# V's scale on GpSimd, and ten score products in one TensorE group

## The chip, the cores and the metric

The program runs on one core of one Trainium2 chip, as a single launch. The metric is the device time of one execution in microseconds, as a median of several runs. The profile is of one further execution. Engines are named as the profile names them: PE (TensorE matmul), PEld (its weight loads), DVE (VectorE), ACT (ScalarE), POOL (GpSimd), SP (SyncE, which issues the DMAs).

## The reference

There are two stages, for 8 batches of 576 positions. The first is causal attention in a window of 128 with 8 heads of 64 and a bias that falls with distance; the second is a gated MLP in which positions are mixed by a matrix.

```
scores = q @ k.T / 8 + slope[h] * -(i - j), kept where 0 <= i - j < 128
attn   = softmax(scores);  x = attn @ v, heads side by side     # 576 x 512 per batch
h      = relu(x @ w_in);   u, v = halves of h                   # 512 each
v_n    = (v - mean(v)) / sqrt(var(v) + 1e-6)
v_s    = w_spatial @ v_n + b_spatial
out    = (u * v_s) @ w_out
```

## The kernel before

**Tiling.** Heads are worked on in pairs (head 2p in partitions 0 to 63, head 2p+1 in 64 to 127), so a batch has four pairs. The 576 positions make five tiles of queries: four of 128 and one of 64. Tile t needs only the keys of tiles t-1 and t, so its scores are 128 wide (tile 0), 256 (tiles 1 to 3) or 192 (tile 4). Batch 1, and the first pair of batch 2, go through another path (`raw_tile`, lines 416 to 487), which the change leaves alone. The other 27 pairs go through `attention(b, p)`, line 500.

**One pair in `attention`.** The scores are fp32 products of 64 rows (L520, one per tile and head), put into PSUM banks tagged "s", of which there are four; two tiles of one head share a bank. `PIECES` cuts them into two groups on PE: tiles 0 to 3 of both heads, and later tile 4, which again takes two "s" banks. DVE adds the bias table and takes the row minimum (L531), ACT takes the exponential and its sum (L537), DVE makes the reciprocals (L545, L549), ACT and DVE split the scaled probabilities into two fp16 halves (L557, L562), and SP issues a DMA transpose of them (L568).

**V's scale.** V is split into two fp16 halves after scaling by a power of two. ACT takes the row sums of |V| (L579, "the abs" below, which writes into the buffer `vl` and into `am`). PE transposes these 128 sums into one row of a PSUM bank tagged "x" (L583), DVE takes the largest and clamps it (L587, L588), PE spreads it to all partitions by two products with a row of constants (L593), DVE makes powers of two of it (L599, L600), and then V is scaled and split (L604 or L607, and L611).

**P times V.** 84 small fp16 products per pair (L624; the trace merges them to 42 rows), in two banks tagged "x", of which there are two in all. ACT and DVE take the result out as two halves of `xt` (L633, L637).

**The MLP of a batch** (`gated`). All its products go through two PSUM banks tagged "m". First five units of v (L689 for a tile of 128, L711 for the tile of 64): relu on ACT (L271) into `vt`, of which there are two buffers, then the statistics on DVE (L650, L654, L655), the power -1/2 on POOL (L659, "the power" below), the scaling on DVE (L663) and the split (L267, L700). Then eight units each of u (L741, 12 products), of the mixing (L762, 14 products; L770 and L776 gate its result) and of the output (L788, 12 products; L267 copies its result out).

**What sets the order.** Nothing is decided at run time. A planner (`Plan`, lines 46 to 135) takes each piece of work with a weight in ns, a due time and its reads and writes, replays them on a clock of its own and writes each engine's queue in that order. Each engine then works its own queue strictly in that order, with semaphores between engines. So work of the attention of one batch stands among the MLP units of the batch before, and a buffer of a tag is handed on in the order in which the pieces were added to the plan.

Of the kernel before, what the change touches and what calls it, by code (L numbers as in the profile page):

```python
# [138 lines left out]
def attn_gmlp_kernel(ctx, tc, qk, v, w_in, w_spT, b_sp, w_out, outT):  # L139
# [48 lines left out]
    def pe(*cols):  # L188
        return sum(11 + n / 2.4 for n in cols)
# [4 lines left out]

    nhalf = fixed([P, 1], F32, "nhalf")
    ident = fixed([P, P], F32, "ident")
    ones = fixed([1, 2 * P], BF16, "ones")
# [26 lines left out]
    def constants():  # L224
        def f():
            nc.gpsimd.iota(relf(), [[-1, 2 * P]], base=P, channel_multiplier=1, allow_small_or_imprecise_dtypes=True)
        plan.add("POOL", 400, 0, f, (), [(relf, 0)])

        def f():
            nc.vector.memset(maskt(), 0.0)  # L230
        plan.add("DVE", dve(256), 0, f, (), [(maskt, 0)])

        def f():
            nc.gpsimd.affine_select(maskt(), maskt(), [[-1, 2 * P]], ALU.is_ge, MASKED, base=P, channel_multiplier=1)
            nc.gpsimd.affine_select(maskt(), maskt(), [[1, 2 * P]], ALU.is_ge, MASKED, base=-1, channel_multiplier=-1)
        plan.add("POOL", 800, 1, f, [(maskt, 0)], [(maskt, 0)])

        def f():
            nc.vector.memset(ident(), 1.0)
            nc.vector.memset(ones()[:, :P], 2.0 ** -12)  # L240
            nc.vector.memset(ones()[:, P:], 2.0 ** -13 / PSC)
            nc.vector.memset(nhalf(), -0.5)
            nc.vector.memset(rstat(), 1.0)
        plan.add("DVE", dve(400), 500, f, (), [(ident, 0), (ones, 0), (nhalf, 0)] + [(rstat, k) for k in range(8)])
# [255 lines left out]
    def attention(b, p):  # L500

        due = FIRST + b * PERIOD - LEAD - (NP - 1 - p) * PERIOD // 4
        st = stat[p % 2]
# [3 lines left out]
        if (b, p) in RAW:  # L507
            xt = plan.buf(work, "xt", 6, [P, 2 * S + R], F32R)
            for t in range(NQ):
                raw_tile(b, p, t, raw, vr, xt, t % 4, due - 6000 + t * 1500)  # L510
            return xt
        for g, banks in enumerate(PIECES):
            sc = [[plan.buf(ps, "s", 4, [P, 2, 2 * P], F32) for _ in range(2)] for _ in banks]
            span = [(k, i, t, min(P, S - t * P), max(0, (t - 1) * P), min(S, (t + 1) * P)) for k, ts_ in enumerate(banks) for i, t in enumerate(ts_)]

            def f(sc=sc, span=span):
                for k, i, t, m, k0, k1 in span:
                    for j in range(2):
                        rows = slice(j * D, (j + 1) * D)
                        nc.tensor.matmul(sc[k][j]()[:m, i, :k1 - k0], raw()[rows, 0, t * P:t * P + m], raw()[rows, 1, k0:k1],  # L520
                                         start=True, stop=True)
            plan.add("PE", SWITCH + pe(*[4 * (x[5] - x[4]) for x in span]), due - 5000 + g * 3000, f, RAWS,
                     [(sc[k][j], i) for k, i, *_ in span for j in range(2)])
            for k, i, t, m, k0, k1 in span:
                for j in range(2):
                    h, n, c0 = 2 * p + j, k1 - k0, P if t == 0 else 0
                    pt = lambda j=j, m=m, t=t, n=n: prob[j]()[:m, OFF[t]:OFF[t] + n]
                    d = due - 4500 + t * 700 + j * 200

                    def f(sc=sc[k][j], pt=pt, i=i, j=j, h=h, t=t, m=m, n=n, c0=c0):  # L530
                        nc.vector.tensor_tensor_reduce(pt(), sc()[:m, i, :n], tabs[h]()[:m, c0:c0 + n], -0.125, 3e38,  # L531
                                                       ALU.add, ALU.min, st()[:m, NM, j, t:t + 1])
                    cols = parts(prob[j], OFF[t], OFF[t] + n)
                    plan.add("DVE", dve(n), d, f, [(sc[k][j], i), (tabs[h], 0)], cols + [(st, (NM, j, t))])

                    def f(pt=pt, j=j, t=t, m=m):
                        nc.scalar.activation(pt(), pt(), AF.Exp, bias=st()[:m, NM, j, t:t + 1], scale=-1.0,  # L537
                                             accum_out=st()[:m, SM, j, t:t + 1])
                    plan.add("ACT", act(n, 2), d, f, cols + [(st, (NM, j, t))], cols + [(st, (SM, j, t))])
        pts = []  # L540
        for j in range(2):
            d = due + j * 1500
# [25 lines left out]
                nc.sync.dma_start_transpose(out=pts[j](), in_=pq[j]().rearrange("p a b -> p (a b)"))  # L568
            plan.add("SP", 3400, d + 1500, f, parts(pq[j], 0, 2 * NB * P), [(pts[j], 0)])


        vh, vl = (plan.buf(work, tag, 2, [P, NQ, P], F16) for tag in ("vh", "vl"))
        am = plan.buf(work, "am", 2, [P, 8], F32)
        one = plan.buf(work, "one", 2, [1, 2], BF16)
        mp = plan.buf(ps, "x", 2, [P, 512], F32)
        d = due - 3000

        def f():
# [1 line left out]
        plan.add("ACT", act(NQ * P, 1), d, f, VRS, [(vl, 0), (am, 0)])  # L580

        def f():
            nc.tensor.transpose(mp()[0:1, 0:P], am()[:, 0:1], ident())  # L583
        plan.add("PE", SWITCH // 2, d + 1, f, [(am, 0), (ident, 0)], [(mp, 0)])

        def f():
            nc.vector.tensor_reduce(one()[:, 0:1], mp()[0:1, 0:P], AX.X, ALU.max)  # L587
            nc.vector.tensor_scalar(one()[:, 0:1], one()[:, 0:1], 2.0 ** -98, 2.0 ** 126, ALU.max, ALU.min)  # L588
        plan.add("DVE", 400, d + 2, f, [(mp, 0)], [(one, 0)])

        def f():
            for k in range(2):
                nc.tensor.matmul(mp()[:, P + k:P + k + 1], ones()[:, k * P:(k + 1) * P], one()[:, 0:1], start=True, stop=True,  # L593
                                 skip_group_check=True)
# [230 lines left out]
    def first(t):  # L825
        for p in range(NP) if t < NQ else ():
            raw_tile(0, p, t, *loads[p], x0[p], p, 2000 + t * 6500 + p * 1500)
        if 0 <= t - 2 < NC_:
            c = t - 2
            win_weights(0, c, UDUE[c], w_u[c])  # L830

    gated(0, x0, first)
    for b in range(1, B):
        xt = []
        for p in range(NP):
            if b == 1 and (b, p) not in RAW and (b, p - 1) in RAW:
                clear()
            xt.append(attention(b, p))
        gated(b, xt)
    plan.emit()  # L840


# [30 lines left out]
```

## Time and profile before

| | |
|---|---|
| median of 3 runs | 648.48 us (648.08 to 651.25) |
| the profiled execution | 648.05 us; its span from first to last instruction 646.3 us |
| granted PE clock, mean | 0.992 of full speed |
| PE busy | 619.0 us, 96% of the span |
| DVE, ACT, POOL busy | 524.2 (81%), 430.9 (67%), 29.6 us (5%) |
| one batch, from the third on | 72.97 us, alike to 0.02 us from batch to batch |

A busy time is the union of an engine's instructions, so it tells how long an engine had something to do and not how well it did it. In the timeline a row gives start, length, engine, line, operation, output and inputs, size and count; rows that follow each other on the same line are merged. Because the rows of PE overlap, what a group costs is read from its start to the start of the next group.

### The profile page before, as it was taken

How to read it: one execution, taken by the hardware profiler on the slowest of the kernel's cores; microseconds unless marked ns; L12 is line 12 of the kernel's file. 1: busy time of each engine (PE TensorE's matmuls, PEld its weight loads, DVE VectorE, ACT ScalarE, POOL GpSimd, SP SyncE). 2: the span in 40 equal slices, each digit the busy share in tenths (PEclk: the TensorE clock that was granted, in tenths of full speed). 3: DMA queues.
4: the chain of work that ended last, by engine and by line, in shares of the span. 5: the costliest groups of instructions: out<-in, count | busy, mean ns of one | idle time of the engine just before them, and what ended most of it. 6: DMA issues, size and time to landing. Idle time of an engine off the chain costs nothing.

```text
span 646.3 us, 14141 instructions
## 1 busy us (share of the span) xinstructions
PE 619.0 (96%) x5037; PEld 529.8 (82%) x5037; DVE 524.2 (81%) x1897; ACT 430.9 (67%) x1322; POOL 29.6 (5%) x53
## 2 busy tenths in 40 slices
PE   4879999999999999999999999999999999999997
PEld 2445688778899879988898979988898978988997
DVE  6999898999887979887887979887887979873632
ACT  4698675989585848686686848676686857662211
POOL 1000010000200010000100010000100010000100
PEclk9998799999999999999999999999999999999999
DMA  7903013799156863778165753858166751733001
GB/s 264 329 20 130 19 62 119 169 209 202 55 132 133 190 107 93 155 155 184 40 143 127 191 112 89 154 152 188 32 154 125 193 113 10 132 79 76 2 20 55
DMA packets 149291, 79.34 MB, mean 123 GB/s; under 512 B 128610, under 2 KB 139874, under 8 KB 149220
## 3 DMA queue, kind: packets, MB, share of 16 engines
q1 hardware_dynamic: 149220, 78.44, 51.8%
q8 instruction: 39, 0.64, 0.4%
q14 instruction: 32, 0.26, 0.1%
HBM read 37.13 MB, written 9.44 MB: 72 GB/s over the span
## 4 chain that ended last, share of the span: by engine, by line
PE 79%; DVE 17%; issue 1%; DMA 1%; ACT 1%; SPq 1%; ACTq 0%; DVEq 0%
PE m L762 16%; PE m L741 16%; PE m L788 14%; PE m L689 13%; PE s L520 8%; PE x L624 6%; DVE pq L562 4%; PE m L711 2%; DVE prob L436 2%; DVE prob L531 2%; DVE gs L298 1%; DMA pt<-in_qk_dram 1%; DVE prob L450 1%; DVE u L770 1%; DVE o L267 1%
## 5 line engine op out<-in xcount | busy, mean ns | idle before, releaser
L537 ACT ACTIVATE prob<-prob,stat 128x128 f32<-128x128 f32 (+1 forms) x270 | 125.4, 466 | 13.6 <-DVE stat L531 12.4
L762 PE MATMUL m<-wsp,vn 128*128 128x288 f32 x768 | 124.3, 299 | 0.7 <-DVE u L770 0.7
L788 PE MATMUL m<-gs,wout 128*128 128x288 f32 x768 | 113.5, 301 | 0.3 <-DVE gs L776 0.2
L762 PEld LDWEIGHTS m<-wsp,vn 128*128 128x128 f32 x768 | 107.5, 188 | 6.7 <-issue 1.9
L557 ACT ACTIVATE pq<-prob,stat 128x128 f16<-128x128 f32 x270 | 103.1, 464 | 12.7 <-ACT prob L537 10.2
L741 PE MATMUL m<-xt,win 128*128 128x288 f32 x768 | 111.6, 298 | 0.0
L788 PEld LDWEIGHTS m<-gs,wout 128*128 128x128 f32 x768 | 103.3, 188 | 7.2 <-issue 1.7
L562 DVE SCALAR_TENSOR_TENSOR pq<-prob,stat,pq 128x128 f16<-128x128 f32 x270 | 104.0, 437 | 4.3 <-ACT pq L557 3.7
L741 PEld LDWEIGHTS m<-xt,win 128*128 128x128 f32 x768 | 103.9, 188 | 4.1 <-issue 2.3
L689 PE MATMUL m<-win,xt 128*128 128x512 f32 x384 | 93.5, 396 | 1.7 <-DVE o L267 1.7
L531 DVE CUSTOM_DVE_ANT_0 prob<-s,tab 128x128 f32<-128x128 f32 (+1 forms) x270 | 89.2, 376 | 2.6 <-PE s L520 2.1
L689 PEld LDWEIGHTS m<-win,xt 128*128 128x128 f32 x384 | 71.5, 189 | 18.2 <-DVE o L267 2.8
L520 PE MATMUL s<-qkraw 64*128 64x256 f32 (+2 forms) x540 | 66.5, 360 | 1.5 <-DVE stat L531 1.3
L770 DVE TENSOR_TENSOR u<-m,u 128x288 f32<-128x288 f32 x64 | 28.9, 451 | 34.2 <-PE m L762 34.2
L520 PEld LDWEIGHTS s<-qkraw 64*128 64x128 f32 (+1 forms) x540 | 42.0, 175 | 16.2 <-issue 9.0
L659 POOL TENSOR_TENSOR st<-st,nhalf 128x1 f32<-128x1 f32 (+1 forms) x40 | 25.6, 640 | 560.4 <-DVE st L655 548.0
L537 ACT ACTIVATION_READ_ACCUMULATOR prob<-prob,stat 128x1 f32 x270 | 50.6, 187 | 0.0
L267 ACT COPY o<-m 128x288 f32<-128x288 f32 x37 | 14.6, 395 | 46.2 <-PE m L788 45.9
L624 PE MATMUL x<-pt,vh 128*64 128x256 f16 (+6 forms) x756 | 41.7, 229 | 0.0
L271 ACT ACTIVATE vt<-m 128x512 f32<-128x512 f32 x31 | 18.5, 598 | 33.0 <-DVE st L654 16.1
L637 DVE SCALAR_TENSOR_TENSOR xt<-x,am,xt 128x288 fp32r<-128x288 f32 x54 | 26.2, 507 | 17.1 <-ACT xt L633 17.0
L624 PEld LDWEIGHTS <-vh 128*64 128x64 f16 x756 | 31.7, 110 | 5.8 <-issue 3.5
(132 smaller groups left out, 820.7 us busy)
## 6 DMA issues: line engine op xcount, KB each, us to landing
qkraw<-in_qk_dram SPq DMA_DIRECT2D x28, 576.0 KB, 3.9
out_dram<-o SPq DMA_DIRECT2D x64, 144.0 KB, 2.0
vraw<-in_v_dram SPq DMA_DIRECT2D x28, 320.0 KB, 2.9
vn<-in_w_in_dram SPq DMA_DIRECT2D x6, 512.0 KB, 7.1
pt<-in_w_out_dram SPq DMA_DIRECT2D x4, 512.0 KB, 4.5
gs<-in_w_spT_dram SPq DMA_DIRECT2D x4, 288.0 KB, 5.0
xt<-in_w_in_dram SPq DMA_DIRECT2D x2, 512.0 KB, 6.8
qkraw<-in_qk_dram SPq DMA_DIRECT2D x3, 320.0 KB, 8.3
```

What stands on the lines that cost most here:

```text
L520: nc.tensor.matmul(sc[k][j]()[:m, i, :k1 - k0], raw()[rows, 0, t * P:t * P + m], raw()[rows, 1, k0:k1], start=True, stop=True)
L531: nc.vector.tensor_tensor_reduce(pt(), sc()[:m, i, :n], tabs[h]()[:m, c0:c0 + n], -0.125, 3e38, ALU.add, ALU.min, st()[:m, NM, j, t:t + 1])
L537: nc.scalar.activation(pt(), pt(), AF.Exp, bias=st()[:m, NM, j, t:t + 1], scale=-1.0, accum_out=st()[:m, SM, j, t:t + 1])
L557: nc.scalar.activation(pq[j]()[:m, 0, cs], prob[j]()[:m, cs], AF.Copy, scale=st()[:m, RC, j, t:t + 1])
L562: nc.vector.scalar_tensor_tensor(pq[j]()[:m, 1, cs], prob[j]()[:m, cs], st()[:m, RC, j, t:t + 1], pq[j]()[:m, 0, cs], ALU.mult, ALU.subtract)
L624: nc.tensor.matmul(xp()[j * D:(j + 1) * D, x0:x0 + n], l()[:, kt, j * D:(j + 1) * D], rhs[:, o:o + n], start=j not in seen, stop=False, sk ...
L637: nc.vector.scalar_tensor_tensor(xt()[:, S + R + hf * HS:S + R + (hf + 1) * HS], xp()[:, :HS], am()[:, 6:7], xt()[:, qs].bitcast(F32), ALU ...
L689: nc.tensor.matmul(pt(), xt[c]()[:, X0[a] + t * P:X0[a] + (t + 1) * P], win()[:, c, w, DH:DF], start=(n == 0), stop=(n == 3 * NC_ - 1))
L741: nc.tensor.matmul(pt()[:, :HS], win()[:, c, w, d * P:(d + 1) * P], xt[c]()[:, X0[a] + hf * HS:X0[a] + (hf + 1) * HS], start=(n == 0), sto ...
L762: nc.tensor.matmul(pt()[:, :HS], l, r, start=(n == 0), stop=(n == len(ops) - 1))
L770: nc.vector.tensor_tensor(u(), pt()[:, :HS], u(), ALU.mult)
L788: nc.tensor.matmul(pt()[:, :HS], wout()[:, d, w, e * P:(e + 1) * P], gs[d]()[:, a, :], start=(n == 0), stop=(n == 3 * ND - 1))
```

## The change

Three things are changed, and the planner's order follows from them.

1. V's scale no longer goes through PE and PSUM. POOL takes the largest of the 128 sums and spreads it, in one instruction (`partition_all_reduce`, weight 4000 in the plan), and DVE does the clamping and the powers of two in four small instructions.
2. From batch 3 on (24 pairs) the ten scores of a pair are one group on PE. Tile 4's two scores go to the two "x" banks, which P times V also uses. The three pairs of batch 2 keep two groups, in "s" banks.
3. The plan adds the scores of pair p+1 ahead of V's scale and P times V of pair p (`AHEAD`), which sets the order in which the "x" banks are handed on.

```diff
-    PIECES = (((0, 1), (2, 3)), ((4,),))
+    BANKS = (((0, 1), ("s", 4)), ((2, 3), ("s", 4)), ((4,), ("x", 2)))
...
-                    d = due - 4500 + t * 700 + j * 200
+                d = due - 4500 + (t if len(banks) < 3 or t < NQ - 1 else -1) * 700 + j * 200
...
+        for g, banks in enumerate((BANKS,) if b >= WHOLE else (BANKS[:2], ((BANKS[2][0], ("s", 4)),))):
+            products(p, due, st, raw, RAWS, g, banks)
...
-            nc.tensor.transpose(mp()[0:1, 0:P], am()[:, 0:1], ident())
-        plan.add("PE", SWITCH // 2, d + 1, f, [(am, 0), (ident, 0)], [(mp, 0)])
-
-        def f():
-            nc.vector.tensor_reduce(one()[:, 0:1], mp()[0:1, 0:P], AX.X, ALU.max)
-            nc.vector.tensor_scalar(one()[:, 0:1], one()[:, 0:1], 2.0 ** -98, 2.0 ** 126, ALU.max, ALU.min)
-        plan.add("DVE", 400, d + 2, f, [(mp, 0)], [(one, 0)])
-
-        def f():
-            for k in range(2):
-                nc.tensor.matmul(mp()[:, P + k:P + k + 1], ones()[:, k * P:(k + 1) * P], one()[:, 0:1], start=True, stop=True,
-                                 skip_group_check=True)
-        plan.add("PE", SWITCH, d + 3, f, [(one, 0), (ones, 0)], [(mp, 1)])
+            nc.gpsimd.partition_all_reduce(am()[:, 1:2], am()[:, 0:1], P, bass.bass_isa.ReduceOp.max)
+        plan.add("POOL", 4000, d + 1, f, [(am, 0)], [(am, 2)])
 
         def f():
             bits = 0x7F800000
-            nc.vector.tensor_scalar(am()[:, 5:7].bitcast(I32), mp()[:, P:P + 2].bitcast(I32), bits, None, ALU.bitwise_and)
+            nc.vector.tensor_scalar(am()[:, 2:3], am()[:, 1:2], 2.0 ** -98, 2.0 ** 126, ALU.max, ALU.min)
+            nc.vector.tensor_scalar(am()[:, 2:3].bitcast(I32), am()[:, 2:3].bitcast(I32), bits, None, ALU.bitwise_and)
+            nc.vector.tensor_scalar(am()[:, 5:7], powers(), am()[:, 2:3], None, ALU.mult)
             nc.vector.tensor_scalar(am()[:, 5:6].bitcast(I32), am()[:, 5:6].bitcast(I32), bits, None, ALU.bitwise_xor)
-        plan.add("DVE", 150, d + 4, f, [(mp, 1)], [(am, 1)])
+        plan.add("DVE", 400, d + 4, f, [(am, 2), (powers, 0)], [(am, 1)])
...
+            todo.append((b, p, scores(b, p)))
+            if len(todo) > AHEAD:
+                rest(*todo.pop(0))
```

The line numbers of the changed kernel are a little higher: L660 there is L659 before, L690 is L689, L712 is L711, L625 is L624, L589 is the abs (L579), L275 is the relu (L271), L271 is the copy (L267), L608 is L607, and L634 and L566 are L633 and L557. The all-reduce is L593 there, and the score products are L514.

How the order moves is seen at three places. The first is POOL's queue over one batch in the middle of the program, before:

```order
L659 TENSOR_TENSOR st<-st,nhalf 128x1
L659 TENSOR_TENSOR st<-st,nhalf 64x1
L659 TENSOR_TENSOR st<-st,nhalf 128x1 x4
L659 TENSOR_TENSOR st<-st,nhalf 64x1
L659 TENSOR_TENSOR st<-st,nhalf 128x1 x4
```

and in the changed kernel:

```order
L660 ISA
L660 TENSOR_TENSOR st<-st,nhalf 128x1
L660 TENSOR_TENSOR st<-st,nhalf 64x1
L660 TENSOR_TENSOR st<-st,nhalf 128x1 x3
L593 ISA
L593 ISA am<-am 128x1 x4
L660 ISA
```

The rows `ISA` without operands are put in by the build: each swaps the library of routines that POOL's cores have loaded, because the power and the all-reduce are in different ones. There is one such row in the program before, ahead of its first iota (L226); the changed program has fourteen more, two for each of seven batches, one behind a batch's fifth power and one ahead of the next batch's first. They wait for no semaphore.

The second place is PE's queue where one batch's outputs end and the next batch's v units begin, before (the first row is the last product of P times V):

```order
L624 MATMUL x<-pt,vl 64x64
L788 MATMUL m<-gs,wout 128x288 x24
L583 MATMUL x<-ident,am 1x128
L689 MATMUL m<-win,xt 128x512 x12
L593 LDWEIGHTS ones
L593 MATMUL x<-one,ones 128x1
L593 LDWEIGHTS ones
L593 MATMUL x<-one,ones 128x1
L711 MATMUL m<-win,xt 128x512 x8
L689 MATMUL m<-win,xt 128x512 x12
```

and in the changed kernel:

```order
L625 MATMUL x<-pt,vl 64x64
L690 MATMUL m<-win,xt 128x512 x12
L712 MATMUL m<-win,xt 128x512 x8
L690 MATMUL m<-win,xt 128x512 x24
L514 MATMUL s<-qkraw 128x128 x2
L514 MATMUL s<-qkraw 128x256 x6
L514 MATMUL x<-qkraw 64x192 x2
L690 MATMUL m<-win,xt 128x512 x12
L625 LDWEIGHTS vh
```

The tiny products are gone, two output units have moved ahead of P times V, and the scores with tile 4 in the "x" banks stand one v unit ahead of the next P times V.

The third place is ACT's queue at the same spot, before:

```order
L633 ACTIVATE xt<-x,am 128x288 x2
L557 ACTIVATE pq_86<-prob_84,stat_87 128x256
L557 ACTIVATE pq_86<-prob_84,stat_87 64x192
L267 COPY xt<-xt 128x64
L579 ACTIVATE vl,am<-vraw 128x640
L267 COPY o<-m 128x288
L271 ACTIVATE vt<-m 128x512
```

and in the changed kernel:

```order
L634 ACTIVATE xt<-x,am 128x288 x2
L566 ACTIVATE pq_86<-prob_84,stat_87 128x256 x2
L271 COPY xt<-xt 128x64
L566 ACTIVATE pq_86<-prob_84,stat_87 64x192
L589 ACTIVATE vl,am<-vraw 128x640
L275 ACTIVATE vt<-m 128x512
L271 COPY vt<-m 64x512
L275 ACTIVATE vt<-vt 64x512
L608 ACTIVATE vh<-vraw,am 128x640
```

The abs still stands right ahead of the first v unit's relu, but a scaling of V (L608) that DVE did there before (L604) now stands on ACT behind that unit.

More of the change, by code (lines that the diff above doesn't have):

```diff
@@ L165, in attn_gmlp_kernel @@
     PERIOD, FIRST, LEAD = 66000, 36000, 18000
+    AHEAD = 1
+    WHOLE = 2
     RAW = {(0, p) for p in range(4)} | {(1, p) for p in range(1)}
@@ L196, in attn_gmlp_kernel @@
     ident = fixed([P, P], F32, "ident")
-    ones = fixed([1, 2 * P], BF16, "ones")
+    powers = fixed([P, 2], F32, "powers")
     tabs = [fixed([P, 2 * P], BF16, f"tab{h}") for h in range(H)]
@@ L239, in f @@
             nc.vector.memset(ident(), 1.0)
-            nc.vector.memset(ones()[:, :P], 2.0 ** -12)
-            nc.vector.memset(ones()[:, P:], 2.0 ** -13 / PSC)
+            nc.vector.memset(powers()[:, 0:1], 2.0 ** -12)
+            nc.vector.memset(powers()[:, 1:2], 2.0 ** -13 / PSC)
             nc.vector.memset(nhalf(), -0.5)
             nc.vector.memset(rstat(), 1.0)
-        plan.add("DVE", dve(400), 500, f, (), [(ident, 0), (ones, 0), (nhalf, 0)] + [(rstat, k) for k in range(8)])
+        plan.add("DVE", dve(400), 500, f, (), [(ident, 0), (powers, 0), (nhalf, 0)] + [(rstat, k) for k in range(8)])
         def f():
@@ L492, in clear, with products, f @@
                      [k for a in range(2) for k in parts(pq[j], a * NB * P + OFF[NQ - 1], (a + 1) * NB * P)])
-    PIECES = (((0, 1), (2, 3)), ((4,),))
+    BANKS = (((0, 1), ("s", 4)), ((2, 3), ("s", 4)), ((4,), ("x", 2)))
     WINDOWS = (((0, 0, 256, 0), (1, 256, 160, 128), (2, 512, 32, 256)),
                ((1, 416, 96, 0), (2, 544, 224, 0), (3, 768, 192, 96), (4, 1024, 64, 224)))
-    def attention(b, p):
+    def products(p, due, st, raw, RAWS, g, banks):
+        SM, NM, RC, TM = range(4)
+        sc = [[plan.buf(ps, *tag, [P, 2, 2 * P], F32) for _ in range(2)] for _, tag in banks]
+        span = [(k, i, t, min(P, S - t * P), max(0, (t - 1) * P), min(S, (t + 1) * P)) for k, (ts_, _) in enumerate(banks) for i, t in enumerate(ts_)]
+        def f():
+            for k, i, t, m, k0, k1 in span:
+                for j in range(2):
+                    rows = slice(j * D, (j + 1) * D)
+                    nc.tensor.matmul(sc[k][j]()[:m, i, :k1 - k0], raw()[rows, 0, t * P:t * P + m], raw()[rows, 1, k0:k1],
+                                     start=True, stop=True)
+        plan.add("PE", SWITCH + pe(*[4 * (x[5] - x[4]) for x in span]), due - 5000 + g * 3000, f, RAWS,
+                 [(sc[k][j], i) for k, i, *_ in span for j in range(2)])
+        for k, i, t, m, k0, k1 in span:
+            for j in range(2):
+                h, n, c0 = 2 * p + j, k1 - k0, P if t == 0 else 0
+                pt = lambda j=j, m=m, t=t, n=n: prob[j]()[:m, OFF[t]:OFF[t] + n]
+                d = due - 4500 + (t if len(banks) < 3 or t < NQ - 1 else -1) * 700 + j * 200
+                def f(sc=sc[k][j], pt=pt, i=i, j=j, h=h, t=t, m=m, n=n, c0=c0):
+                    nc.vector.tensor_tensor_reduce(pt(), sc()[:m, i, :n], tabs[h]()[:m, c0:c0 + n], -0.125, 3e38,
+                                                   ALU.add, ALU.min, st()[:m, NM, j, t:t + 1])
+                cols = parts(prob[j], OFF[t], OFF[t] + n)
+                plan.add("DVE", dve(n), d, f, [(sc[k][j], i), (tabs[h], 0)], cols + [(st, (NM, j, t))])
+                def f(pt=pt, j=j, t=t, m=m):
+                    nc.scalar.activation(pt(), pt(), AF.Exp, bias=st()[:m, NM, j, t:t + 1], scale=-1.0,
+                                         accum_out=st()[:m, SM, j, t:t + 1])
+                plan.add("ACT", act(n, 2), d, f, cols + [(st, (NM, j, t))], cols + [(st, (SM, j, t))])
@@ L502, in attention, with scores @@
+    def scores(b, p):
         due = FIRST + b * PERIOD - LEAD - (NP - 1 - p) * PERIOD // 4
@@ L510, in attention @@
                 raw_tile(b, p, t, raw, vr, xt, t % 4, due - 6000 + t * 1500)
[L511 to L527, printed above, removed]
-                    d = due - 4500 + t * 700 + j * 200
[L530 to L539, printed above, removed]
+            return lambda: xt
+        for g, banks in enumerate((BANKS,) if b >= WHOLE else (BANKS[:2], ((BANKS[2][0], ("s", 4)),))):
+            products(p, due, st, raw, RAWS, g, banks)
         pts = []
@@ L569, in attention @@
             plan.add("SP", 3400, d + 1500, f, parts(pq[j], 0, 2 * NB * P), [(pts[j], 0)])
+        return lambda: attention(p, due, vr, VRS, pts)
+    def attention(p, due, vr, VRS, pts):
         vh, vl = (plan.buf(work, tag, 2, [P, NQ, P], F16) for tag in ("vh", "vl"))
         am = plan.buf(work, "am", 2, [P, 8], F32)
-        one = plan.buf(work, "one", 2, [1, 2], BF16)
-        mp = plan.buf(ps, "x", 2, [P, 512], F32)
         d = due - 3000
@@ L830, in first, with rest @@
             win_weights(0, c, UDUE[c], w_u[c])
+    xts = []
+    def rest(b, p, f):
+        xts.append(f())
+        if p == NP - 1:
+            gated(b, [xts.pop(0) for _ in range(NP)])
     gated(0, x0, first)
+    todo = []
     for b in range(1, B):
-        xt = []
         for p in range(NP):
@@ L837, in attn_gmlp_kernel @@
                 clear()
-            xt.append(attention(b, p))
-        gated(b, xt)
+            todo.append((b, p, scores(b, p)))
+            if len(todo) > AHEAD:
+                rest(*todo.pop(0))
+    while todo:
+        rest(*todo.pop(0))
     plan.emit()
```

## Prediction

> **What bounds the kernel now.** I read the page's busy times first (they stand in the table above), then a table of stretches (one batch, from its first power to the next batch's), then PE's timeline inside that batch, then the waits.
>
> ```profile
> 378.56:451.53 72.97, 72.54 (x621) 63.57 (x620) 61.04 (x224) 52.13 (x163) 3.17 (x6) 1.00 0.58 133
> ```
>
> The columns are the stretch and its length, then busy time of PE, PEld, DVE, ACT and POOL, PE's clock and the DMA share. PE is busy for 72.54 of 72.97 us at full clock: a batch lasts as long as PE's queue does, so a us taken from that queue is a us gained as long as nobody comes late. DVE follows with 61.04 us, and POOL has 3.17. The waits of PE on DVE for a bank are short today (engine, line, releaser, total us, times, longest):
>
> ```profile
> PE m L689 <- DVE o L267: 1.7, 4, 0.4
> PE s L520 <- DVE stat L531: 1.3, 2, 0.8
> ```
>
> **Part 1: what leaves PE.** A group's cost is read from its start to the next start.
>
> ```profile
> 325.44 0.56 PE L762 MATMUL m<-wsp,vn 128*128 128x288 f32 x3
> ...
> 327.28 1.75 PE L741 MATMUL m<-xt,win 128*128 128x288 f32 x12
> ...
> 342.00 0.27 PE L583 MATMUL x<-ident,am 128*1 128x128 f32 x1
> 342.03 0.65 PE L762 MATMUL m<-wsp,vn 128*128 128x288 f32 x3
> ...
> 344.06 0.20 PE L593 MATMUL x<-one,ones 1*128 1x1 bf16 x2
> 344.19 1.86 PE L788 MATMUL m<-gs,wout 128*128 128x288 f32 x12
> 345.98 1.79 PE L520 MATMUL s<-qkraw 64*128 64x128 f32 x16
> 347.70 1.85 PE L788 MATMUL m<-gs,wout 128*128 128x288 f32 x12
> ...
> 352.88 0.54 PE L520 MATMUL s<-qkraw 64*64 64x192 f32 x4
> 353.36 1.86 PE L788 MATMUL m<-gs,wout 128*128 128x288 f32 x12
> ```
>
> ```profile
> 309.04 5.78 PE L689 MATMUL m<-win,xt 128*128 128x512 f32 x24
> 314.74 1.79 PE L520 MATMUL s<-qkraw 64*128 64x128 f32 x16
> ...
> 368.63 3.44 PE L788 MATMUL m<-gs,wout 128*128 128x288 f32 x24
> 371.91 0.27 PE L583 MATMUL x<-ident,am 128*1 128x128 f32 x1
> 372.61 3.03 PE L689 MATMUL m<-win,xt 128*128 128x512 f32 x12 [0.43 <-DVE o L267]
> 375.58 0.20 PE L593 MATMUL x<-one,ones 1*128 1x1 bf16 x2
> 375.71 2.11 PE L711 MATMUL m<-win,xt 128*128 128x512 f32 x8
> 377.65 1.54 PE L689 MATMUL m<-win,xt 128*128 128x512 f32 x6
> ```
>
> First, what a change of shape costs at its ends. An output unit between two other shapes takes 345.98 - 344.19 = 1.79 us (a unit and two ends). Two units behind P times V and ahead of L583 take 371.91 - 368.63 = 3.28 us (two units and one end, since L583 turns out to cost the unit ahead of it nothing). So a unit is 1.59 us and an end 0.10 us. A mixing unit among its like takes 327.28 - 325.44 = 1.84 us, but 344.06 - 342.03 = 2.03 us between L583 and L593: 0.10 is L593's end, 0.09 belongs to L583.
>
> - L583: 342.03 - 342.00 = 0.03, and 0.09 in the unit behind, 0.12 us.
> - L593: 344.19 - 344.06 = 0.13, and two ends, 0.33 us; where it touches a score group (one pair in four in this batch) only 0.13. Mean 0.28 us.
> - Both for 27 pairs: 27 x 0.40 = 10.8 us.
> - Tile 4 as a group of its own: 353.36 - 352.88 = 0.48 and two ends, 0.68 us. In the large group it costs its columns: the 16 rows of tiles 0 to 3 take 347.70 - 345.98 = 1.72 us for 896 columns per head, so 192 columns take 0.37 us. Saved 0.31 us, less where a tiny product shares the end: 0.28 us x 24 pairs = 6.7 us.
>
> Together 17.5 us, all of it on the path. The DVE instructions of V's scale stay four small ones, so I count nothing there; they are covered by DVE's 11.9 idle us per batch, and if that cover were gone they would cost what they cost before. DMAs: none is added, and the order of SP's queue moves outputs and loads of q, k and v past each other by a place or two; I count nothing, since the DMA engines are busy for 0.58 of the batch.
>
> **Part 2: tile 4 in the "x" banks.** P times V of one pair now waits until DVE has read tile 4's scores of the next pair, and those scores wait until P times V of the pair before has been taken out. In the v stage the order leaves one v unit between the scores and P times V. Nothing like it is in the trace. Below: nothing, since two output units moved ahead of P times V loosen another wait. Above: the longest wait of PE on DVE, 0.8 us, for each of 24 pairs, 19 us. I take one mean wait per batch (1.7 + 1.3 over 6 waits, 0.5 us) for six batches: 3 us, because DVE has a sixth of its time free and tile 4 is put first in its queue.
>
> **Part 3: POOL's two swaps of library.** This decides the sign. Each batch's queue is now: five powers, swap, four all-reduces, swap. The second swap starts when the last all-reduce ends and stands ahead of the next batch's first power. Behind that power waits DVE's scaling L663, and behind L663 all of DVE's queue. The rows at that place, from ACT, DVE and POOL:
>
> ```profile
> 372.38 0.73 ACT L579 ACTIVATE vl<-vraw 128x640 f16<-128x640 f32 x1
> 373.02 0.19 ACT L579 ACTIVATION_READ_ACCUMULATOR vl<-vraw 128x1 f32 x1
> ...
> 375.68 0.60 ACT L271 ACTIVATE vt<-m 128x512 f32<-128x512 f32 x1 [2.19 <-PE m L689]
> ```
>
> ```profile
> 379.15 0.55 DVE L663 TENSOR_SCALAR vt<-vt,st 128x512 f32<-128x512 f32 x1
> ...
> 380.68 0.67 DVE L700 TENSOR_TENSOR vn<-vt,vn 128x512 fp32r<-128x512 f32 x1
> ```
>
> ```profile
> 378.56 0.55 POOL L659 TENSOR_TENSOR st<-st,nhalf 128x1 f32<-128x1 f32 x1 [60.95 <-DVE st L655]
> ```
>
> The abs ends at 373.21, 4.6 us behind the end of P times V (368.63), and ACT's order there has not changed. In the changed order the first v unit starts right at the end of P times V; call that 0. The power starts no earlier than 4.6 + R + S, with R the all-reduce and S the swap. Unit 1's `vt` is free at L700's end, 381.35 - 378.56 = 2.8 us behind the power's start, and then unit 3's relu takes 0.6. PE needs that relu's bank for unit 5, which it reaches after 2.97 (372.61 to 375.58), 1.94 (L711), 5.70 (309.04 to 314.74) and the joined scores (1.72 + 0.37): 12.7 us. So PE loses 4.6 + R + S + 3.4 - 12.7 = S + R - 4.7 us per batch, and nothing below that. The last batch has no scores in that place: 2.1 us more.
>
> R: nearest is the power on the same 128x1 operand, 0.55 us; I take 0.6, with 0.3 and 1.0 as ends, other POOL rows. S is in no row as a number of its own. What there is:
>
> ```profile
> 0.90 0.34 POOL L226 IOTA u<- 128x256 f32 x1 [0.39 <-POOLq L861]
> ```
>
> ```profile
> vn<-in_w_in_dram SPq DMA_DIRECT2D x6, 512.0 KB, 7.1
> pt<-in_w_out_dram SPq DMA_DIRECT2D x4, 512.0 KB, 4.5
> gs<-in_w_spT_dram SPq DMA_DIRECT2D x4, 288.0 KB, 5.0
> xt<-in_w_in_dram SPq DMA_DIRECT2D x2, 512.0 KB, 6.8
> qkraw<-in_qk_dram SPq DMA_DIRECT2D x3, 320.0 KB, 8.3
> ```
>
> The only swap of before sits ahead of the iota, which idled 0.39 us: the lower end. But the program before needs one library only, so that swap may have found it loaded by the execution before. [...] I take the mean of the three that landed among other traffic, (7.1 + 6.8 + 8.3) / 3 = 7.4 us, because these swaps come in the middle of transfers too. Then PE loses 7.4 + 0.6 - 4.7 = 3.3 us in six batches and 5.4 in the last, 25 us. DVE comes out of the stall with its queue late, and PE's next waits (P times V behind the scores) come on top: 0.5 us, the mean wait above, in seven batches, 3.5 us.
>
> The first swap, behind the fifth power, delays the next all-reduce; its DVE instructions stand far behind in DVE's queue, behind the next scores, so I count nothing. If that cover is thin, it costs up to S once more.
>
> [...]
>
> **Sum.** Against the profiled execution (648.05 us: span 646.3 and 1.75 around it; 0.07% below the median of 648.48): - 17.5 + 3 + 25 + 3.5 = + 14, so 662 us, slower by 2.2%.
>
> **Rivals.**
> - *The swap costs next to nothing* (0.39 us, as ahead of the iota). Parts 1 and 2 alone: 648 - 17.5 + 3 = 633.5 us, faster. It holds as long as S + R stays under 4.7. For it: the one row with a swap. [...] Chance 0.18.
> - *It comes out even.* With S midway between the 5.0 and the 6.8 row, 5.9 us, the swap costs 6 x 1.8 + 3.9 = 14.7 us, with 1.7 for the waits behind: 650 us. Chance 0.10. [...]
> - *The "x" banks bind.* 19 us in place of 3, with a free swap: 650 us; PE's waits would then be on L531 at L624, not at L689. For it: DVE's share rises as a batch gets shorter. Chance 0.04.
> - *The swap costs more than any landing here, or the first swap is exposed too.* With 8.3 + 1.0, 6 x 4.6 + 6.7 = 34 us, and the "x" banks at their upper 19: 684 us. Chance 0.14.
> - My forecast, from 655 to 675 us: 0.54.
>
> **How the numbers follow.** The range is 634 to 684: it begins where the swap is free (half of that rival lies below) and ends at the dearest sum; what is left out is some 0.09 below and 0.08 above. About 0.5%, 3.2 us, is what a measurement of this kernel can tell from no change. Faster: 0.18 and a little of the even case, 0.20. Same: the rest of the even case and the "x" banks, 0.10. Slower: 0.70.
>
> **What would show it.** In the profile after: no L583 and L593 group, score groups of 20 rows on PE that take about 2.1 us, and output units in runs. The all-reduce rows on POOL near 0.6 us, with a gap of about 7 us between the last one and the next power that no DVE row explains. DVE idle ahead of L663 on POOL, some 4 to 5 us in each of seven batches, and PE idle on ACT ahead of the fifth v unit, some 3 us. A batch of about 75 us. The forecast is wrong if that gap on POOL is under 4 us, or if the fifth v unit does not wait.

## The result, and the profile after

The changed kernel takes 666.4 us (median of 4, 665.62 to 667.13), the kernel before 649.44 us in the same comparison (median of 4): ratio 1.0259, 95% interval 1.0227 to 1.0291, slower by 17 us. The profiled execution is the one of 667.13 us, its span 665.4 us. Line numbers below are those of the changed kernel: the power is L660, DVE's scaling behind it L664, the all-reduce L593, the v units on PE L690, the u units L742, the mixing units L763, the scores L514, P times V L625.

One batch, from its first power to the next, in the table of stretches (columns as before: PE, PEld, DVE, ACT, POOL, clock, DMA share):

```profile
396.11:471.05 74.94, 70.66 (x604) 63.18 (x602) 62.40 (x226) 51.29 (x160) 4.64 (x10) 0.98 0.56 129
```

Before, PE worked through 72.54 of 72.97 us. Now it has less to do, 70.66 us even with a lowered clock in it, and the batch is 2 us longer: PE waits for 4.3 us. The waits (engine, line, releaser, total us, times, longest) say on whom:

```profile
POOL st L660 <- issue: 43.9, 6, 7.8
DVE vt L664 <- POOL st L660: 28.1, 6, 5.5
PE m L690 <- ACT vt L275: 15.7, 6, 3.4
PE m L763 <- DVE u L276: 3.0, 3, 1.0
PE m L742 <- DVE u L276: 2.0, 2, 1.0
```

The first and the third did not stand in the list before, and the second was short there:

```profile
DVE vt L663 <- POOL st L659: 3.1, 7, 0.4
```

Read downwards they are one chain, six times: POOL stands still ahead of a power in a time for which the profile has only two instructions of 83 ns (`MODIFY_POOL_CONFIG`, right behind the last all-reduce), DVE waits for that power, ACT's relu for DVE's `vt` buffer, and PE for the bank that this relu empties. POOL's timeline at one of the six places, and ahead of the next batch's all-reduces:

```profile
387.51 0.75 POOL L593 PARTITION_ALL_REDUCE am<-am  x1 [14.28 <-ACT vl L589]
396.11 0.59 POOL L660 TENSOR_TENSOR st<-st,nhalf 128x1 f32<-128x1 f32 x1 [7.85 <-issue]
...
407.97 0.55 POOL L660 TENSOR_TENSOR st<-st,nhalf 128x1 f32<-128x1 f32 x1 [2.23 <-DVE st L656]
414.36 0.44 POOL L593 PARTITION_ALL_REDUCE am<-am  x1 [5.84 <-ACT pq L566]
```

Between the last all-reduce and the first power POOL is idle for 7.85 us here, and for 6.97 to 7.36 us at the five other places: this is the second swap. Between the fifth power and the next all-reduce it is 5.84 us here, 5.68 to 6.13 in all six: the first swap. The list names an instruction of ACT for these, but the abs that the all-reduce needs had ended 2.6 to 5.7 us ahead of it in all six (at 411.77 here). The all-reduce itself is short:

```profile
L593 POOL PARTITION_ALL_REDUCE am<-am x27 | 15.3, 566 | 335.8 <-ACT vl L589 200.2
```

Of the two swaps the one ahead of the powers is the longer (6.97 to 7.85 us, against 5.68 to 6.13 ahead of the all-reduces), and it is the one that stands in the way.

What PE does at the stall, in its timeline and in the stretches around it (clock third from the end):

```profile
321.17 0.54 PE L514 MATMUL x<-qkraw 64*64 64x192 f32 x4
323.97 4.46 PE L690 MATMUL m<-win,xt 128*128 128x512 f32 x12 [2.26 <-ACT vt L275]
...
334.47 5.05 PE L742 MATMUL m<-xt,win 128*128 128x288 f32 x36 [1.04 <-DVE u L276]
```

```profile
321.00:324.00 3.00, 0.74 (x9) 0.22 (x5) 2.52 (x7) 1.22 (x2) 0.42 (x1) 1.00 0.11 21
324.00:328.40 4.40, 4.40 (x14) 3.04 (x16) 4.30 (x13) 2.50 (x7) 0.73 (x2) 0.64 0.56 200
```

The fifth v unit comes 2.26 us late. It then takes 4.46 us where a unit like it took 3.03 before, because the granted clock is 0.64 behind the wait. And 10 us later PE waits 1.04 us more on DVE, which is still behind. Together 2.26 + 1.43 + 1.04 = 4.7 us in this batch.

### The profile page after: what moved, and what is told of

It reads as the page before. It is cut to its first block, busy times and chain, and to the rows that moved or that the text cites. A ratio compares the mean times of both kernels' runs of the same rounds, so it can differ in the third digit from the quotient of the medians.

```text
span 665.4 us, 14031 instructions
## 1 busy us (share of the span) xinstructions
PE 616.1 (93%) x4956; PEld 532.9 (80%) x4956; DVE 532.7 (80%) x1921; ACT 422.4 (63%) x1298; POOL 42.8 (6%) x80
## 5 line engine op out<-in xcount | busy, mean ns | idle before, releaser
L531 ACT ACTIVATE prob<-prob,stat 128x256 f32<-128x256 f32 (+2 forms) x270 | 125.5, 467 | 41.5 <-DVE stat L525 41.5
L763 PE MATMUL m<-wsp,vn 128*128 128x288 f32 x768 | 120.9, 297 | 4.6 <-DVE u L276 3.0
L690 PE MATMUL m<-win,xt 128*128 128x512 f32 x384 | 104.6, 430 | 17.1 <-ACT vt L275 15.7
L763 PEld LDWEIGHTS m<-wsp,vn 128*128 128x128 f32 x768 | 107.3, 188 | 7.6 <-DVE u L276 3.7
L742 PE MATMUL m<-xt,win 128*128 128x288 f32 x768 | 110.1, 297 | 2.0 <-DVE u L276 2.0
L690 PEld LDWEIGHTS m<-win,xt 128*128 128x128 f32 x384 | 79.2, 209 | 38.1 <-ACT vt L275 17.8
L789 PE MATMUL m<-gs,wout 128*128 128x288 f32 x768 | 109.2, 298 | 0.4 <-DVE u L771 0.4
L742 PEld LDWEIGHTS m<-xt,win 128*128 128x128 f32 x768 | 103.9, 188 | 4.9 <-DVE u L276 2.8
L566 ACT ACTIVATE pq<-prob,stat 128x128 f16<-128x128 f32 x270 | 103.8, 466 | 4.6 <-DVE stat L558 2.2
L525 DVE CUSTOM_DVE_ANT_0 prob<-s,tab 128x256 f32<-128x256 f32 (+2 forms) x222 | 75.6, 379 | 1.1 <-PE s L514 0.7
L514 PE MATMUL s<-qkraw 64*128 64x256 f32 (+2 forms) x444 | 52.7, 372 | 4.1 <-DVE stat L525 4.1
L531 ACT ACTIVATION_READ_ACCUMULATOR prob<-prob,stat 128x1 f32 (+1 forms) x270 | 51.1, 189 | 0.0
L514 PEld LDWEIGHTS s<-qkraw 64*128 64x128 f32 (+1 forms) x444 | 37.6, 191 | 13.4 <-DVE stat L525 6.1
L664 DVE TENSOR_SCALAR vt<-vt,st 128x512 f32<-128x512 f32 (+1 forms) x40 | 21.5, 538 | 28.4 <-POOL st L660 28.1
L625 PE MATMUL x<-pt,vh 128*64 128x256 f16 (+6 forms) x756 | 41.8, 230 | 0.0
L271 ACT COPY o<-m 128x288 f32<-128x288 f32 x32 | 12.7, 397 | 41.5 <-PE m L789 37.6
L660 POOL TENSOR_TENSOR st<-st,nhalf 128x1 f32<-128x1 f32 (+1 forms) x40 | 23.7, 593 | 230.1 <-DVE st L656 168.2
L593 POOL PARTITION_ALL_REDUCE am<-am x27 | 15.3, 566 | 335.8 <-ACT vl L589 200.2
L625 PEld LDWEIGHTS <-vh 128*64 128x64 f16 x756 | 31.7, 110 | 6.2 <-issue 6.2
```

Of the source, the lines that this page charges most:

```text
L566: nc.scalar.activation(pq[j]()[:m, 0, cs], prob[j]()[:m, cs], AF.Copy, scale=st()[:m, RC, j, t:t + 1])
L625: nc.tensor.matmul(xp()[j * D:(j + 1) * D, x0:x0 + n], l()[:, kt, j * D:(j + 1) * D], rhs[:, o:o + n], start=j not in seen, stop=False, sk ...
L660: nc.gpsimd.tensor_tensor(st()[:m, 11:12], st()[:m, 10:11], nhalf()[:m], ALU.pow)
L690: nc.tensor.matmul(pt(), xt[c]()[:, X0[a] + t * P:X0[a] + (t + 1) * P], win()[:, c, w, DH:DF], start=(n == 0), stop=(n == 3 * NC_ - 1))
L742: nc.tensor.matmul(pt()[:, :HS], win()[:, c, w, d * P:(d + 1) * P], xt[c]()[:, X0[a] + hf * HS:X0[a] + (hf + 1) * HS], start=(n == 0), sto ...
L763: nc.tensor.matmul(pt()[:, :HS], l, r, start=(n == 0), stop=(n == len(ops) - 1))
```

## The experiments

Theory 1: the power's lateness behind the second swap is the whole loss, and the rest of the change gains some 13 us. Rivals: the joint group of scores with its shared banks costs; the all-reduces themselves make DVE and PE late; a swap costs wherever it stands.

One means is used in six of the runs: a plain copy on GpSimd in the power's place works on the same tile and has the same waits and place in every queue, but needs no swap: in batches 2 to 4 of the run a_copy6 it starts 0.90 to 1.29 us behind the end of the last all-reduce, as soon as DVE's statistics are there, where the power of the changed kernel starts 6.97 to 7.85 us behind it. It leaves out the power -1/2, so the result is not the reference's. Times are medians, and each ratio is to the kernel before in the same comparison.

**No swaps: the power replaced by a copy (a_copy), and the same in the kernel before (b_copy).**

```diff
-            nc.gpsimd.tensor_tensor(st()[:m, 11:12], st()[:m, 10:11], nhalf()[:m], ALU.pow)
+            nc.gpsimd.tensor_copy(st()[:m, 11:12], st()[:m, 10:11])
```

> The changed kernel with GpSimd's power (L660) replaced by a plain copy of the variance on GpSimd: same operands, same waits, same order on every engine, but the copy needs no reload of GpSimd's routines (the result is then not the reference's: the normalised values are scaled by the variance instead of one over its root). Theory 1 (the reload behind the last all-reduce of a batch delays the first power, and through DVE's L664 the fifth v unit on PE, six times): the last batch, which has no such stall, took 2.7 us less than its like before, so the other six should go from about 75.0 to about 70.3: 666.4 - 6 x 4.8 = 637.6, say 633 to 641, and DVE's wait ahead of L664 on POOL falls from 28 us to under 3. Rival 2 (the joint score group and the shared banks are what costs): stays above 655. Rival 3 (the all-reduces themselves delay DVE and PE): stays above 655.

> Control: the kernel before with the same replacement (power by a plain copy on GpSimd, result not the reference's). No reload stands in that kernel between powers, so theory 1 expects no change from the replacement itself: 647 to 650, at most 0.3 us a batch if the copy is shorter than the power's 0.59 us. If it were faster by 5 us or more, the gain of the other run would be partly the power's own.

Measured: 644.13 us, ratio 0.9923 (0.9897 to 0.9948), and for the control 650.46 us, 1.001 (0.9994 to 1.0026). The copy itself brings nothing, and without swaps the slower kernel is a faster one: both rivals that said "above 655" fall. But 644 is 6 us above what theory 1 gave. The first rows of POOL's timeline show one thing that was new there, and the waits what hung on it:

```profile
8.39 0.34 POOL L230 IOTA u<- 128x256 f32 x1 [7.88 <-issue]
```

```profile
DVE tab L265 <- POOL u L239: 9.3, 1, 9.3
```

With only copies left, the program ends with the all-reduce's routines loaded, and the next launch starts with a swap of 7.88 us ahead of the iota, from which all tables are made. In the changed kernel the wait of DVE on these tables is 2.0 us.

**The copy in batches 1 to 6 only (a_copy6)**, so that the last batch's powers leave their routine loaded.

```diff
-            nc.gpsimd.tensor_tensor(st()[:m, 11:12], st()[:m, 10:11], nhalf()[:m], ALU.pow)
+            nc.gpsimd.tensor_copy(st()[:m, 11:12], st()[:m, 10:11]) if 0 < b < B - 1 else nc.gpsimd.tensor_tensor(st()[:m, 11:12], st()[:m, 10:11], nhalf()[:m], ALU.pow)
```

> The changed kernel with the power replaced by a copy in batches 1 to 6 only (result then not the reference's); the last batch keeps the power, so that the launch ends with the power's routine resident, as it does before the change. In the run with copies everywhere GpSimd's first instruction came 7.9 us late (the routine left behind by the launch before had to be replaced at the start), and PE was some 5 us behind by 100 us. Theory 1: without the six stalls and without that late start 637 to 641. Rival (the missing 6 us lie in the joint score group or the shared banks): 643 to 646 again.

Measured: 636.94 us, ratio 0.9804 (0.9778 to 0.9831). Two swaps remain, behind batch 0's powers and ahead of batch 7's. POOL's iota is back at 1.15 us, and a batch has no stall:

```profile
374.14:444.38 70.24, 69.86 (x609) 62.74 (x609) 62.32 (x226) 51.14 (x160) 2.37 (x9) 1.00 0.61 135
```

So everything in the change but the swaps that were taken out gains 650.24 - 636.94 = 13.3 us, and these cost 666.4 - 636.94 = 29.5 us, 4.9 us for each of six batches. (The two times are from different comparisons, in which the kernel before took 649.44 and 650.24 us.)

**A delay without a swap (a_delay20, a_delay40)**: the kernel with copies in batches 1 to 6, and memsets behind the last all-reduce ahead of a batch's copies.

```diff
             nc.gpsimd.partition_all_reduce(am()[:, 1:2], am()[:, 0:1], P, bass.bass_isa.ReduceOp.max)
+            for _ in range(20 if p == 1 else 0): nc.gpsimd.memset(idle(), 0.0)
```

> The same kernel as the one with copies in batches 1 to 6, with 20 memsets of 128x150 on GpSimd behind the all-reduce of pair p == 1, the last ahead of a batch's first copy: GpSimd is busy there for about half as long as a reload (some 3 to 4 us), and nothing is reloaded. Theory 1 (only lateness of the first power counts, and PE has about 4.7 us in hand): at most 0.5 us a batch, 639 to 644. Rival (whatever GpSimd does there costs in proportion): 3.5 of 7.4 us, so about half of the loss of 27 us, 651 to 654.

> The same with 40 memsets, about as long as a reload (6 to 8 us). Theory 1: the stall is back without any reload, the time near that of the changed kernel: 660 to 670, with DVE's wait ahead of L664 on GpSimd 4 to 6 us in each of six batches. Rival (it is the reload itself that costs, by what it moves or holds up, not the lateness): within 3 us of the kernel without memsets.

Measured: 654.11 us, ratio 1.007 (1.0046 to 1.0095), and 694.15 us, 1.0686 (1.0651 to 1.0721). By its time the first run stands at the edge of the rival's bracket, and the second is far above theory 1's. But the delays were not the ones named: a memset took 0.28 us where 0.15 to 0.2 were counted, so they are 5.64 and 11.26 us:

```profile
234.71 0.74 POOL L593 PARTITION_ALL_REDUCE am<-am  x1 [14.29 <-ACT vl L589]
235.32 5.64 POOL L594 MEMSET idle<- 128x150 f32 x20
240.91 0.18 POOL L661 COPY st<-st 128x1 f32<-128x1 f32 x1
```

```profile
247.74 0.41 POOL L593 PARTITION_ALL_REDUCE am<-am  x1 [14.30 <-ACT vl L589]
248.02 11.26 POOL L594 MEMSET idle<- 128x150 f32 x40
259.23 0.18 POOL L661 COPY st<-st 128x1 f32<-128x1 f32 x1
```

The lateness that they did make still tells the theories apart. It is read batch by batch, because a seventh pair, in batch 1, has memsets too: with 40 of them PE waits there once for 8.47 us, and for 1.96 without, so the whole times overstate what the six places cost. The table has the mean of batches 2 to 5, from the timelines of POOL: from the start of the last all-reduce to the start of the first power or copy, and from one batch's first power or copy to the next batch's.

| | all-reduce to power or copy | a batch | lost |
|---|---|---|---|
| copies, no memsets | | 70.32 us | |
| 20 memsets | 6.01 us | 72.86 us | 2.53 us |
| 40 memsets | 11.56 us | 78.61 us | 8.29 us |
| the changed kernel, with its swaps | 7.92 us | 75.28 us | 4.96 us |

The line through the two memset runs, (8.29 - 2.53) / (11.56 - 6.01) = 1.04 us per us, gives 4.5 us at 7.92. The power also takes 0.41 us longer than the copy (0.59 against 0.18), which makes it 4.9. The swap loses 4.96: within what a line through two runs can tell, it costs what any work of that length costs in that place, and nothing is left over for what it loads. The line meets zero at 3.6 us, so by this line about that much lateness is free. A cost in proportion to the time, fixed by the swap's 4.96 at 7.92, would be 3.8 at 6.01 and 7.2 at 11.56: too much at the one and too little at the other. That the reload costs by what it moves or holds up, wherever it stands, is not borne out; the run with 40 memsets loses more than the swaps do and reloads nothing there.

The two runs also show in which order the cover gives way. With 20 memsets PE hardly waits at the fifth v unit, but, in batches 3 and 5, at a u unit 8 us later, whose bank DVE empties late, and the clock stays at 1.00 (in batches 2, 4 and 6 there are two waits of 1.01 us instead). With 40 it waits at the fifth v unit, and the clock is 0.50 over the unit behind (timelines of PE):

```profile
317.03 3.03 PE L691 MATMUL m<-win,xt 128*128 128x512 f32 x12
...
327.52 5.05 PE L743 MATMUL m<-xt,win 128*128 128x288 f32 x36 [2.19 <-DVE u L276]
```

```profile
341.13 5.49 PE L691 MATMUL m<-win,xt 128*128 128x512 f32 x12 [5.63 <-ACT vt L275]
```

**V's scale alone, with its swaps (a_scale)**: the scores go as before.

```diff
-    WHOLE = 2
+    WHOLE = 99
```

> V's scale on GpSimd alone (the scores as before, in two PE groups and the s banks). Theory 1: the reloads still stall six batches, and the gain of the joint group (6.7 us less about 3 us of waits) is missing: 668 to 673. Rival 2 (shared banks and joint group cost): below 655, since V's scale alone then gains about 10 us.

Measured: 706.56 us, ratio 1.0879 (1.0833 to 1.0926), 34 us above the bracket. The expectation left out what this edit does to the order: without the joint group an all-reduce falls in between the fourth and the fifth power, so there are four swaps a batch, two of them ahead of a power:

```profile
341.98 0.71 POOL L660 TENSOR_TENSOR st<-st,nhalf 128x1 f32<-128x1 f32 x1 [0.53 <-DVE st L656]
348.50 0.38 POOL L593 PARTITION_ALL_REDUCE am<-am  x1 [5.81 <-DVE stat L525]
355.83 0.59 POOL L660 TENSOR_TENSOR st<-st,nhalf 128x1 f32<-128x1 f32 x1 [6.95 <-issue]
```

```profile
POOL st L660 <- issue: 78.6, 11, 7.7
DVE vt L664 <- POOL st L660: 59.3, 12, 7.5
PEld m L763 <- ACT u L275: 34.1, 5, 7.4
```

Twice the stalls, 12 where the whole change has 6. PE's six longest waits, of 6.1 to 7.0 us, stand at the mixing units now (five) and at a score group (one). The joint group made little of its own (below), but its order kept the all-reduces together.

**V's scale alone, without swaps (a_scale6)**: both edits, `WHOLE = 99` and copies in batches 1 to 6.

> V's scale on GpSimd alone (scores as before, in two groups and the s banks), with copies instead of powers in batches 1 to 6 (result not the reference's), so without the four reloads a batch that took the kernel with V's scale alone to 706.6 us. Theory 1: what leaves PE by V's scale, 0.40 x 27 = 10.8 us, is gained: 649.9 - 10.8 = 639, say 637 to 645; the joint score group is then worth the difference to the run with both (5 us or less). Rival (the all-reduce makes DVE and PE late in itself): 648 or more.

Measured: 637.27 us, ratio 0.9815 (0.9781 to 0.9849). Beside the 636.94 us with both parts, the joint group is worth 0.3 us, less than these runs can tell from nothing.

**The scores alone (a_scores)**: V's scale over PE as before, the joint group and the shared banks as in the change.

> The scores' part alone: the joint group of ten scores with the last tile in the x banks, V's scale over PE as before. By the terms of the prediction 649.9 - 6.7 + 3 = 646; by the two runs with copies no change, 648 to 651; if sharing the x banks with V's scale and P times V costs more than the group saves, over 653.

Measured: 647.85 us, ratio 0.9978 (0.9965 to 0.9992), between the two forecasts and a little faster than before. A score group in the kernel with copies shows why it is so little:

```profile
327.84 1.79 PE L514 MATMUL s<-qkraw 64*128 64x128 f32 x16
329.56 0.54 PE L514 MATMUL x<-qkraw 64*64 64x192 f32 x4
330.03 0.67 PE L763 MATMUL m<-wsp,vn 128*128 128x288 f32 x3
```

Tiles 0 to 3 take 1.72 us and tile 4 takes 330.03 - 329.56 = 0.47 us, as much as it took as a group of its own (0.48). Only the two ends are saved.

**The last pair over PE (a_last)**: pair p == 1, whose all-reduce is the last ahead of a batch's powers, takes its scale the old way, and the others stay on GpSimd.

```diff
+        if p == 1:
+            ... (one, mp, transpose, reduce, two products and DVE's bits, as before)
+        else:
             nc.gpsimd.partition_all_reduce(am()[:, 1:2], am()[:, 0:1], P, bass.bass_isa.ReduceOp.max)
```

> As the changed kernel, but the pair p == 1, whose all-reduce is the last ahead of a batch's powers, takes its scale the old way over PE; GpSimd then turns back to the power's routine some 15 us earlier. Theory 1: the reload is hidden in all batches, the stall goes, and 7 of the 27 pairs give back their 0.40 us: about 637.6 + 2.8 = 640, say 636 to 645, faster than before by 1%. A rival by which any reload in a batch costs (by what it holds up on GpSimd, wherever it stands): 660 or more.

Measured: 640.29 us, ratio 0.9859 (0.9826 to 0.9892). Every batch still swaps twice, but the swap back has 20 us:

```profile
355.55 0.35 POOL L622 PARTITION_ALL_REDUCE am<-am  x1 [12.52 <-ACT vl L592]
376.32 0.60 POOL L689 TENSOR_TENSOR st<-st,nhalf 128x1 f32<-128x1 f32 x1 [20.42 <-DVE st L685]
```

The first power waits for DVE's statistics again, as before the change. Against the run with copies this is 3.4 us more, what seven pairs are worth at the 650.24 - 637.27 = 13.0 us that 27 pairs gained with V's scale alone, so nothing is left that the swaps could cost. This computes the reference in full and is 1.4% faster than the kernel before: a swap costs by where it stands.

**All pairs on GpSimd, the last all-reduce earlier (a_own)**: pair p == 1 gets buffers of its own, so that its all-reduce comes ahead of pair 0's; that of pair 2 is held behind the powers.

```diff
-        am = plan.buf(work, "am", 2, [P, 8], F32)
+        am = plan.buf(work, *(("am1", 1) if p == 1 else ("am", 2)), [P, 8], F32)
+        out = junk if p == 1 else vl
...
-            nc.scalar.activation(vl(), vr(), AF.Abs, accum_out=am()[:, 0:1])
+            nc.scalar.activation(out(), vr(), AF.Abs, accum_out=am()[:, 0:1])
...
-        plan.add("POOL", 4000, d + 1, f, [(am, 0)], [(am, 2)])
+        plan.add("POOL", 4000, d + 1, f, [(am, 0)] + ([(last[-1], 2)] if p == 2 else []), [(am, 2)])
```

> The whole change with one thing moved, nothing left out: pair p == 1 gets its own one-buffer tile for the maximum and its own 640-byte tile for the absolute values nobody reads, so its absolute values and its all-reduce no longer wait for the pair two before it, and come before those of pair p == 0. The last all-reduce ahead of a batch's powers is then pair 0's, some 15 us before the first power, and GpSimd can turn back to the power's routine in that time. Theory 1: all 27 scales on GpSimd and no stall: 636 to 641, like the kernel with copies (636.9), and no wait of DVE's L664 on GpSimd. Rival (each reload costs wherever it stands): 655 or more.

Measured: 643.35 us, ratio 0.9903 (0.9882 to 0.9924), 2 us above the bracket. The second swap is hidden in every batch, and a batch in the middle takes 70.39 us, like the 70.24 with copies. The rest lies ahead of batch 2. The planner's order differs there (the first power of batch 1 comes at 167.43 us, against 163.74 with copies; why was not taken apart further), and in batch 1 it is the first swap that shows, on DVE and then on PE. POOL stands still for 7.45 us there, between the fifth power and the all-reduce at 188.69, whose abs had ended at 178.14:

```profile
189.10 0.15 DVE L599 TENSOR_SCALAR am<-am 128x1 f32<-128x1 f32 x1 [3.21 <-POOL am L594]
```

```profile
190.32 0.66 PE L765 MATMUL m<-wsp,vn 128*128 128x288 f32 x3 [3.29 <-DVE u L276]
```

**The same with the scores as before (a_own_scale)**: `WHOLE = 99` on top of it.

> The same with the scores as before (two groups, s banks). By the terms of the prediction the joint group is worth 6.7 us less 3 us of waits, so 3.7 us slower than the run with it; by the two runs with copies (636.94 with it, 637.27 without) nothing: within 2 us of it.

Measured: 654.24 us, ratio 1.0067 (1.0042 to 1.0093), 11 us above the run with the joint group, and neither forecast. One DVE wait on a power is left in it, of 0.5 us. The order has moved the next all-reduce, and DVE's instructions behind it, close behind the fifth power; from batch 3 on the first swap is exposed, and at 6.77, 7.06 and 6.85 us in three batches it is longer than in the changed kernel, though the abs had ended by the fifth power (timelines of POOL, DVE and PE):

```profile
321.58 0.55 POOL L662 TENSOR_TENSOR st<-st,nhalf 128x1 f32<-128x1 f32 x1 [1.12 <-DVE st L658]
328.90 0.38 POOL L594 PARTITION_ALL_REDUCE am<-am  x1 [6.77 <-ACT pq L566]
```

```profile
329.31 0.15 DVE L599 TENSOR_SCALAR am<-am 128x1 f32<-128x1 f32 x1 [1.70 <-POOL am L594]
```

```profile
336.50 0.67 PE L765 MATMUL m<-wsp,vn 128*128 128x288 f32 x3 [1.95 <-DVE u L773]
```

That accounts for some 2 of the 4 us by which a batch is longer here (74.6 against 70.4). Behind this wait of 1.95 us, which comes at the same place in three batches, PE's clock fell in two (0.71 over 336.50 to 340.00, 0.57 over 484.26 to 488.00) and stayed at 1.00 in the one between; those two take 74.61 and 74.77 us, the one between 73.08. So the clock is another 1.6 us where it falls, and some 0.6 us are left open.

## Why the prediction was right, and by how much each step was off

The forecast was 662 us, slower by 2.2%; it is 666.4, slower by 2.6%, inside the forecast's own 655 to 675, by the mechanism named. The rivals of a free swap (0.39 us) and of an even end (5.9 us) fell with the gap of 6.97 to 7.85 us. The one of a dearer swap fell with the same gap, under 8.3 us, and with DVE's wait on an all-reduce, 1.5 us, once. "The x banks bind" fell with the 636.94 us without swaps. The mechanism was right; that the sum came within 5 us is in part luck, because terms that were too large and too small nearly cancel. Step by step:

- *What leaves PE, 17.5 us.* L583 and L593 were counted at 10.8 us. Their rows from start to next start add up to 6.0 + 3.4 = 9.4 us in the kernel before, 2.6 of it waits that end at the row behind L583; V's scale alone without swaps gained 650.24 - 637.27 = 13.0 us. What else went along was not taken apart. The term for the joint group was too large: tile 4 was counted at its columns, 0.37 us, and takes 0.47. What is left are its two ends, 0.20 us for a pair, at most 4.8 us where 6.7 stood.
- *The x banks, 3 us.* P times V takes 42.5 us from start to start in the kernel with copies, 1.1 of it waits of PE, and 40.6 before: 1.9 us. In the run with the scores alone it is 50.6, 8.1 of it waits, but there L583 also shares these banks and its own rows fall from 6.0 to 0.8. The joint group and its banks come out at a gain of 0.3 to 1.8 us where 3.7 was predicted.
- *Without swaps, 14.5 us faster than before*, was the sum of both: 13.3 measured.
- *S = 7.4 and R = 0.6.* The gap is 6.97 to 7.85, the all-reduce 0.566. Right in size, but the way there was luck: 7.4 was a mean of landings of transfers, and no run shows that a swap has to do with one. What the runs show in its place is that gap, and the same swap took 6.84 to 7.69 us at six places of the run with V's scale alone where the DMA engines were busy for 0.05 of the gap or less (7.69 us from 430.38 on, at 0.00). No trace shows what the swap does in that time.
- *PE loses S + R - 4.7, 3.3 us in six batches.* The wait at the fifth v unit is 2.23 to 3.43 us, 15.7 us in six, 2.6 in the mean. At the place shown above, the last all-reduce starts 3.2 us behind the end of P times V (312.40 against 309.17) where 4.6 stood, and PE starts 3.9 us behind the power (323.97 against 320.08) where 3.4 stood. Two losses stand behind the wait. The clock's fall costs 1.4 to 1.6 us (4.46 to 4.61 for 3.03) in each, 9.2 in six; the working took PE at full clock throughout. And what is late next was sized at 0.5 us and is 1.0 in five of the six, 5.1. These three add up to 30.0 us, against the 29.5 that the swaps cost by the run without them.
- *The last batch, 5.4 us.* It has no stall. Its last all-reduce stands 32 us ahead of the first power, since no next batch's pairs come in between, and the swap is hidden. This error, the wait's size and the missed clock nearly cancel, which is luck: 25 + 3.5 = 28.5 us predicted, 29.5 measured.
- *The first swap, nothing.* Right for this order: DVE's wait on an all-reduce is 1.5 us, once. The two runs with the all-reduces moved show how thin that cover is.

Of the signs named ahead, the all-reduce near 0.6 us, the gap near 7, DVE's wait of 4 to 5 us (28.1 in six), PE's of some 3 us and the batch of about 75 us (75.3 in the mean of batches 2 to 5) are there; the score group is 2.19 us instead of 2.1, and there are six stalls and not seven.

## What to carry to other kernels

Where an engine changes between routines that have to be loaded, count the loads in its order of instructions and price each at the place where it stands: here the same two swaps a batch cost 29.5 us where the powers follow the last all-reduce closely, and nothing that can be seen with 20 us of room. A planner that has no price for them will put them anywhere, and an edit elsewhere (here the scores) can double them, so read the order again after each edit. And a wait on PE costs more than its length where the clock falls behind it: 1.4 to 1.6 us more here, behind waits of 2.23 to 3.43 us.

## What was not expected of the hardware

- The routine that one launch leaves loaded is there for the next: the iota waits 0.65 us where the launch ends with the power's routine, and 7.88 us where it ends with the all-reduce's (644.13 against 636.94 us, with the copies of the first and the last batch as the only other difference).
- How long a swap takes is not one number. In the changed kernel it is 5.68 to 6.13 us to the all-reduce's routines and 6.97 to 7.85 us back. But the way there took 6.77 to 7.06 us in three batches of the last run and 7.45 us in one of the run before it, so the direction alone does not set it. Nor does other traffic alone: with V's scale alone the way back took 6.84 to 7.69 us at DMA shares of 0.05 or less, and in the changed kernel 6.97 to 7.85 us at 0.57 to 0.74. What does is open.
- PE's clock fell behind waits of 2.23 to 3.43 us at the fifth v unit, in six of six (0.63 to 0.65 over the unit behind), and stayed at 1.00 behind the two of 2.19 us at a u unit, with 20 memsets. Behind the wait of 5.63 us, with 40 memsets, it was 0.50 over the unit behind. But the length of the wait does not decide alone: in the last run it fell behind two waits of 1.95 us and not behind a third of the same length at the same place. What else decides is not shown.
